# A choice product on 64 columns, and a last block computed in two halves, in an attention and expert kernel

## The chip, the cores and the metric

The kernel runs on one core of a Trainium2 chip. The metric is the device time of one execution in microseconds (us). The time before is 420.47 us, the median of 3 runs (420.36 to 421.25).

## The reference

For each of 8 batches there are 8 heads with 576 tokens of 64 values, and 32 "packs". Two softmax attentions come first: packs over keys and values, then queries over the packed result. Their output, 576 tokens of 512 values for each batch, goes into a layer of 8 experts.

```
p_packed = sm_attn(p, k, v)
x        = sm_attn(q, p_packed, p_packed)          # [8, 576, 512] after the heads are joined
logits   = x @ w_gate;  local = sigmoid(x @ w_local)
for each batch, token after token:
    fresh = argmax(logits[s])
    e     = fresh if s == 0 or local[s] < 0.5 else the token before's e
    out[s] = softmax(logits[s])[e] * (relu(x[s] @ w1[e]) @ w2[e])
```

`w1` is 512 x 1024 and `w2` 1024 x 512 for each expert.

## The kernel before

Batches run one after the other, with the attention of later batches woven between the expert products of the current one. The expert of a batch's first token is found early and its `w1` and `w2` are loaded by an address in a register. The whole batch is computed with that expert; tokens that need another one are counted as strays, and a block behind a branch (L1259, not entered here unless there are strays) repairs them. So every engine loads the count (L1258, a load into a register), compares and branches at L1259, and then runs the closing waits (L1346).

**The choice product.** For batches 2 to 7 `first_choice` (L715 to L743) takes the attention of token 0, normalizes it, turns it with one DVE transpose into the tile `first`, and multiplies it on TensorE with the gate weights (L737): two matmuls in float32, one for each Q (group of four heads). Each is two instructions in the profile, each with its own weight load. The stationary operand is `first[:, Q:Q + 4]`, four slots of 32 columns, of which only the first column matters: the one row of `ep` that is read is row 0. `first` has NQ + 3 = 5 slots, so that four are there from Q = 1; the last three are zero for good (memset at L257).

**The expert layer.** For each batch there are two halves of tokens, and in each half 8 chunks of 128 hidden columns. `layer1` makes a chunk's hidden values (L1013: six matmuls of 320 or 256 columns), `relu` splits them into a high and a low part (ACT L1024, DVE L1028), and `layer2` multiplies them with the chunk's `w2` (three matmuls for a block of 128 tokens: high by high, high by low, low by high, L1041, all of 512 columns). `BLOCKS` names the blocks of a half: 0, 1 and the mixed block 4 (L1046, L1050) in the first, 2 and 3 in the second. Each block has one PSUM bank that accumulates over the 8 chunks. Chunk c's second layer follows chunk c + 1's first layer.

**The end.** In the last half of the last batch the chunks before last and last are ordered by block: block 2 of both, then block 3 of both (L1138). When a block is complete, `store` scales it by the gate (block 2 on DVE, L1076; block 3 on ACT, L1074) and issues its DMA: on the queue of SP, except block 3 of the last batch, which goes on ACT's (L1085). The count of strays (`count_strays`) is put in ahead of these matmuls.

**What orders the work.** The program's order is written out when the kernel is built: `weave` keeps a model of the engines' clocks (`Clock`) and takes, step by step, the generator whose data are due. A matmul's price goes by its output columns; it is priced as a small tile, with a charge for the change, if it has 64 or fewer rows on one side and its output has not exactly 64 rows (L108). `hold` keeps free PSUM banks back for the blocks of a half that begins (L1115). All engines run their instructions in this order. Lines that the change touches: L37, L256, L738, L1034 to L1050, L1055 to L1087, L1104, L1115, L1131, L1138.

Of the kernel before, what the change touches and what calls it, by code (L numbers as in the profile page):

```python
# [8 lines left out]
F32 = mybir.dt.float32  # L9
# [13 lines left out]
NQ = H // HQ  # L23
# [10 lines left out]
WIDE = GROUP * 5  # L34
ROWS = ((0, 128), (128, 128), (WIDE, 128), (WIDE + 128, 128), (256, TAIL))
BLOCKS = ((0, 1, 4), (2, 3))

RATIO, BACKLOG, CREDIT, DEBT, AHEAD = 0.7, 800.0, 1000.0, 1300.0, 2

# [132 lines left out]
def packed_attn_moe_kernel(  # L172
# [80 lines left out]
    for x in v_rest + a_rest:  # L253
        nc.gpsimd.memset(x[TAIL:128], 0.0)

    first = const.tile([128, NQ + 3, 32], F32, name="first")  # L256
    nc.gpsimd.memset(first, 0.0)  # L257
    some = const.tile([1, 1], I32, name="some")
    v0_all = const.tile([128, B], F32, name="v0_all")
# [118 lines left out]
    def begin(b, st, early=False):  # L378
        st["b"], st["early"] = b, early

        st["second"] = isinstance(b, int) and b == 1
        st["pairs"] = st["early"] or st["second"]
        st["pick"] = isinstance(b, int) and b < PICK
        st["gate"] = gate_all[b % 3 if isinstance(b, int) else 0]
        st["ppT"] = [None] * NQ
        st["wp"], st["w2s"], st["at"] = [], [], b if isinstance(b, int) else -1
        st["quads"] = [0, 0]
        st["wq"] = st["passed"] = st["asked"] = st["scored"] = st["weighed"] = st["valued"] = st["raised"] = st["peeked"] = 0
# [326 lines left out]
    def first_choice(st, sT):  # L715

        m, nm, sm = (tile_([128, NQ], F32, x) for x in ("em", "enm", "esm"))
        yield need(*sT.values())
        for Q in range(NQ):
            nc.vector.reduce_max(out=m[:, Q:Q + 1], in_=sT[Q][:, 0, 0], axis=AX.X)  # L720
        nc.vector.tensor_scalar(out=nm, in0=m, scalar1=-SCALE, scalar2=None, op0=ALU.mult)
        yield need(nm)
        es = tile_([128, NQ, 32], F32, "es")
        for Q in range(NQ):
            nc.scalar.activation(
                out=es[:, Q], in_=sT[Q][:, 0, 0], func=AF.Exp, bias=nm[:, Q:Q + 1], scale=SCALE, accum_out=sm[:, Q:Q + 1],
            )
        st["peeked"] = 1
        yield need(es, sm)
        nc.vector.tensor_scalar(out=sm, in0=sm, scalar1=1e-9, scalar2=None, op0=ALU.add)  # L730
        nc.vector.reciprocal(out=sm, in_=sm)
        nc.vector.tensor_tensor(out=es, in0=es, in1=sm.unsqueeze(2).broadcast_to([128, NQ, 32]), op=ALU.mult)
        nc.vector.transpose(out=first[:, 0:NQ].rearrange("a q n -> a (q n)"), in_=es.rearrange("a q n -> a (q n)"))
        yield need(first, st["gs"], banks=1)
        ep = bank()
        for Q in range(NQ):
            nc.tensor.matmul(  # L737
                out=ep[:, 0:GW], lhsT=first[:, Q:Q + 4].rearrange("a q n -> a (q n)"), rhs=st["gs"][:, Q, 0:GW],  # L738
                start=(Q == 0), stop=(Q == NQ - 1),
            )  # L740
        yield need(ep)
        yield from first_code(st, ep[0:1, 0:E])
        give(ep)  # L743
# [276 lines left out]
    def relu(t, half, h, done):  # L1020
# [10 lines left out]
        give(t)  # L1031
        done.add("h")

    def layer2(c, h, w, st, i):  # L1034
        if c == 0:
            st["acc", i] = bank()
        acc = st["acc", i]
        if i < 4:
            hs = [h[:, x + 128 * (i % 2):x + 128 * (i % 2) + 128] for x in (0, WIDE + TAIL)]
            for n, (hi, wi) in enumerate(((0, 0), (0, 1), (1, 0))):  # L1040
                nc.tensor.matmul(  # L1041
                    out=acc, lhsT=hs[hi], rhs=w[:, wi],
                    start=(c == 0 and n == 0), stop=(c == NC - 1 and n == 2),
                )
        else:
            nc.tensor.matmul(  # L1046
                out=acc, lhsT=h[:, 256:WIDE + TAIL], rhs=w[:, 0],
                start=(c == 0), stop=False, skip_group_check=True,
            )
            nc.tensor.matmul(  # L1050
                out=acc[0:TAIL], lhsT=h[:, 256:WIDE], rhs=w[:, 1],
                start=False, stop=(c == NC - 1), skip_group_check=True,
            )

    def store(b, st, i, mask=None):  # L1055

        acc, pe = st["acc", i], st["pe"]
        yield need(acc)
        o = tile_([128, DM], F32, "o")
        row, rows = ROWS[i]  # L1060
        if i == 4:

            o2 = tile_([TAIL, DM], F32, "o2", "o")
            nc.scalar.activation(out=o2, in_=acc[TAIL:128], func=AF.Copy, scale=pe[TAIL:128, i:i + 1])
            yield need(o2)
            nc.vector.scalar_tensor_tensor(
                out=o[:TAIL], in0=acc[0:TAIL], scalar=pe[0:TAIL, i:i + 1], in1=o2, op0=ALU.mult, op1=ALU.add,
            )
        elif i == 0:

            nc.scalar.activation(out=o[:, 0:256], in_=acc[:, 0:256], func=AF.Copy, scale=pe[:, i:i + 1])
            nc.vector.tensor_scalar(out=o[:, 256:DM], in0=acc[:, 256:DM], scalar1=pe[:, i:i + 1], scalar2=None, op0=ALU.mult)
        elif i == 3:
            nc.scalar.activation(out=o, in_=acc, func=AF.Copy, scale=pe[:, i:i + 1])  # L1074
        else:
            nc.vector.tensor_scalar(out=o, in0=acc, scalar1=pe[:, i:i + 1], scalar2=None, op0=ALU.mult)  # L1076
        give(acc)
        dst = at(out, b)[row:row + rows]
        if mask is not None:
            new, o = o, tile_([128, DM], F32, "o")  # L1080
            nc.sync.dma_start(out=o[:rows], in_=dst)
            nc.vector.copy_predicated(
                out=o[:rows], mask=mask[:rows, i:i + 1].broadcast_to([rows, DM]), data=new[:rows],
            )
        queue = nc.scalar if isinstance(b, int) and b == B - 1 and i == 3 else nc.sync  # L1085
        clock.rate = 300.0
        queue.dma_start(out=dst, in_=o[:rows])  # L1087

    def chunks(todo, aside, mask=None):

        def second(last, blocks):
            b, st, half, c, h, done = last
            for i in blocks:
                yield need(h, *st["w2s"][c:c + 1], banks=1 if c == 0 else 0, first=True,
                           when=lambda: "h" in done and len(st["w2s"]) > c and (c < NC - 1 or "pe" in st))
                yield need(st["w2s"][c])
                layer2(c, h, st["w2s"][c], st, i)
                if c == NC - 1:  # L1100
                    aside(store(b, st, i, mask))
            if c == 0:
                hold[0] = 1
            if half == 1 and i == BLOCKS[half][-1]:  # L1104
                give(st["w2s"][c])

        last = None
        for b, st in todo:
            for half in range(2):
                for c in range(NC):  # L1110
                    if c % 2 == 0:
                        yield need(when=lambda: st["wq"] > c // 2 and st["quads"][half] == NQ)
                    if c == 0:
                        at_batch[0] = b
                        hold[0] = 1 + len(BLOCKS[half])  # L1115
                    hi, lo = (x[:, 0, 256 * (c % 4 // 2) * st["early"]:] for x in st["wp"][c // 4])
                    if mask is None and (b, half, c) == (0, 0, 2):
                        give(warm_ps)
                    yield need(hi, lo, *(x[:, WIDE * half:WIDE * half + 256] for y in ("a2h", "a2l") for x in st[y]), banks=1, first=True)
                    h, done = tile_([128, 2 * WIDE], F32R, "h"), set()  # L1120
                    aside(relu(layer1(c, half, st), half, h, done))
                    st["begun"] = True
                    st["passed"] += 1
                    if half == 1:
                        if c % 4 == 3:
                            give(*st["wp"][c // 4])
                        if c == NC - 1:
                            give(*st["a2h"], *st["a2l"])
                    end = half == 1 and c == NC - 1 and b is todo[-1][0]
                    if last is not None and not end:  # L1130
                        yield from second(last, BLOCKS[last[2]])  # L1131
                    before, last = last, (b, st, half, c, h, done)

        if mask is None:
            ending.append(True)
            yield need()
            aside(count_strays())
        for x, blocks in ((before, (2,)), (last, (2,)), (before, (3,)), (last, (3,))):  # L1138
            yield from second(x, blocks)

    def count_strays():

# [208 lines left out]
```

## Time and profile before

| | |
|---|---|
| median of 3 runs | 420.47 us (420.36 to 421.25) |
| the profiled execution | 422.95 us, its span 421.1 us |
| granted TensorE clock | 0.999 |
| busy: PE, PEld, DVE, ACT, POOL | 97%, 77%, 70%, 43%, 11% of the span |
| instructions | 10055 |

The profile shows one execution. PE is TensorE's matmul track, PEld its weight loads, which run beside matmuls; DVE is VectorE, ACT ScalarE, POOL GpSimd, SP the engine that issues most DMAs. A letter q behind an engine marks its queue or sequencer: DMA issues, waits, branches. A matmul's duration holds the time through the array, so matmuls in a row overlap in the record, and the distance of their starts tells what one costs.

### The profile page before, as it was taken

Reading aid. Unit: us, or ns where it says so; the run is one execution under the profiler, and the core shown is the slowest. Engines: PE = TensorE matmul, PEld = TensorE weight load, DVE = VectorE, ACT = ScalarE, POOL = GpSimd, SP = SyncE. Lnnn points to the kernel's source line nnn. Section 1 sums busy time; section 2 is a strip of 40 time slices with the busy share of each in tenths; the row PEclk is TensorE's granted clock in tenths of the full one; section 3 lists DMA queues with packets and bytes.
Section 4 is the critical chain, followed back from the end, with each engine's and each line's share of the span. In section 5 each row is a group of like instructions: output and inputs, shape, how many; then the busy total and the mean of one; then the engine's idle time right before and its main releaser. Section 6 shows DMA issues by size and latency. Waiting matters only on the chain.

```text
span 421.1 us, 10055 instructions
## 1 busy us (share of the span) xinstructions
PE 409.9 (97%) x3810; PEld 322.3 (77%) x3816; DVE 296.3 (70%) x915; ACT 181.6 (43%) x443; POOL 46.9 (11%) x66
## 2 busy tenths in 40 slices
PE   6999999999999999999999999999999999999995
PEld 3656677867887788878887788877887788878883
DVE  1587458796596968978496978978497987765221
ACT  2464553456244644254244643354343653453221
POOL 2003320253102000200003000300003000300000
PEclk9999999999999999999999999999999999999999
DMA  7859993999996699938986599929997500823021
GB/s 205 250 180 321 258 129 94 307 161 220 139 188 238 208 167 139 324 86 243 133 171 261 198 173 130 333 81 247 128 146 296 150 2 2 296 93 125 0 65 58
DMA packets 161160, 73.11 MB, mean 174 GB/s; under 512 B 125768, under 2 KB 141128, under 8 KB 161104
## 3 DMA queue, kind: packets, MB, share of 16 engines
q1 hardware_dynamic: 160624, 72.04, 74.9%
q8 instruction: 32, 0.52, 0.6%
q10 hardware_dynamic: 480, 0.35, 0.3%
q14 instruction: 24, 0.20, 0.2%
HBM read 62.94 MB, written 9.44 MB: 172 GB/s over the span
## 4 chain that ended last, share of the span: by engine, by line
PE 87%; DMA 8%; SPq 2%; DVE 1%; issue 1%; ACT 1%; DVEq 0%; ACTq 0%
PE bank L1041 40%; PE bank L1013 23%; PE bank L1046 4%; PE bank L1050 3%; DMA qn<-in_q_dram 3%; PE bank L971 3%; PE bank L560 2%; DMA kv<-in_q_dram 2%; PE bank L496 2%; PE bank L534 2%; PE bank L611 2%; DMA w1t<-in_moe_w_dram 2%; DMA qt<-in_k_dram 2%; PE bank L801 1%; PE bank L226 1%; PE bank L441 1%
## 5 line engine op out<-in xcount | busy, mean ns | idle before, releaser
L1041 PE MATMUL bank<-w2s,h 128*128 128x512 f32 x768 | 205.3, 399 | 0.2 <-ACT h L1024 0.2
L1041 PEld LDWEIGHTS bank<-w2s,h 128*128 128x128 f32 x768 | 135.8, 188 | 29.3 <-ACT wph L983 5.0
L1028 DVE SCALAR_TENSOR_TENSOR h<-bank,h 128x256 fp32r<-128x256 f32 x192 | 61.4, 347 | 61.4 <-ACT h L1024 60.2
L1024 ACT ACTIVATE h<-bank 128x256 fp32r<-128x256 f32 (+1 forms) x128 | 52.7, 412 | 114.0 <-PE bank L1013 112.2
L1013 PEld LDWEIGHTS bank<-a2h,wph 128*128 128x128 f32 x256 | 46.6, 188 | 16.7 <-issue 2.8
L1013 PE MATMUL bank<-a2h,wph 128*128 128x320 f32 (+1 forms) x256 | 57.0, 303 | 0.1
L1013 PE MATMUL bank<-a2h,wpl 128*128 128x320 f32 (+1 forms) x256 | 55.9, 298 | 0.5 <-DVE wpl L986 0.5
L676 POOL TENSOR_TENSOR a2l<-a2t,a2h 128x576 fp32r<-128x576 f32 (+2 forms) x17 | 23.3, 1376 | 294.8 <-ACT a2h L673 294.8
L1013 PE MATMUL bank<-a2l,wph 128*128 128x320 f32 (+1 forms) x256 | 54.5, 294 | 0.0
L999 ACT CAST w2s<-w2raw 128x512 fp32r<-128x512 f32 x64 | 39.0, 625 | 7.6 <-DMA w2raw<-in_moe_w_dram 7.6
L1013 PEld LDWEIGHTS bank<-a2h,wpl 128*128 128x128 f32 x256 | 40.9, 188 | 1.5 <-DVE wpl L986 1.5
L1013 PEld LDWEIGHTS bank<-a2l,wph 128*128 128x128 f32 x256 | 41.0, 188 | 0.0
L1001 DVE TENSOR_TENSOR w2s<-w2raw,w2s 128x512 fp32r<-128x512 f32 x50 | 33.2, 681 | 2.9 <-ACT w2s L999 2.9
L1046 PE MATMUL bank<-w2s,h 128*128 128x512 f32 x64 | 26.9, 420 | 0.0
L1050 PE MATMUL bank<-w2s,h 128*64 128x512 f32 x64 | 25.2, 393 | 0.0
L983 ACT CAST wph<-bank 128x512 fp32r<-128x512 f32 x28 | 15.2, 600 | 22.3 <-PE bank L971 22.3
L1001 POOL TENSOR_TENSOR w2s<-w2raw,w2s 128x512 fp32r<-128x512 f32 x14 | 18.2, 1308 | 25.0 <-ACT w2s L999 17.3
L631 DVE STREAM_TRANSPOSE sT<-bank 128x288 f32<-128x288 f32 (+2 forms) x36 | 13.2, 418 | 9.0 <-ACT gate L629 8.5
L504 DVE TENSOR_SCALAR_CACHE_REDUCE a<-bank 128x288 f32<-128x288 f32 x32 | 13.3, 453 | 7.3 <-PE bank L496 7.3
L986 DVE TENSOR_TENSOR wpl<-bank,wph 128x512 fp32r<-128x512 f32 x28 | 18.4, 680 | 0.0
L595 DVE STREAM_TRANSPOSE qn<-qn 128x1152 f32<-128x1152 f32 x12 | 16.3, 1361 | 0.0
L463 DVE STREAM_TRANSPOSE qn<-qn 128x1152 f32<-128x1152 f32 x12 | 16.3, 1360 | 0.0
(161 smaller groups left out, 462.9 us busy)
## 6 DMA issues: line engine op xcount, KB each, us to landing
w2raw<-in_moe_w_dram SPq DMA_DIRECT2D x64, 256.0 KB, 6.6
w1t<-in_moe_w_dram SPq DMA_DIRECT2D x14, 1024.0 KB, 5.2
kv<-in_v_dram SPq DMA_DIRECT2D x16, 512.0 KB, 5.9
out_dram<-o SPq DMA_DIRECT2D x31, 256.0 KB, 3.2
qn<-in_k_dram SPq DMA_DIRECT2D x24, 288.0 KB, 6.7
qn<-in_q_dram SPq DMA_DIRECT2D x24, 288.0 KB, 7.2
w1t<-in_moe_w_dram SPq DMA_DIRECT2D x4, 512.0 KB, 5.2
kw<-in_k_dram SPq DMA_DIRECT2D x3, 512.0 KB, 7.2
```

What stands on the lines that cost most here:

```text
L463: nc.vector.transpose(out=kT, in_=kT)
L595: nc.vector.transpose(out=qT, in_=qT)
L676: eng.tensor_tensor(out=a2l, in0=a2t, in1=a2h.bitcast(F32), op=ALU.subtract)
L986: nc.vector.tensor_tensor(out=lo[fh][:, Q], in0=ts[fh, Q], in1=hi[fh][:, Q].bitcast(F32), op=ALU.subtract)
L999: nc.scalar.copy(out=w[:, 0], in_=raw)
L1001: (nc.gpsimd if st["pick"] and not st["early"] or st["early"] and c > 1 else nc.vector).tensor_tensor(out=w[:, 1], in0=raw, in1=w[:, 0].bi ...
L1013: nc.tensor.matmul(out=t[:, :GROUP * (m1 - m0)], lhsT=st["wp"][c // 4][wi][:, Q, fs], rhs=a2[ai][Q][:, GROUP * m0:GROUP * m1], start=(n == ...
L1024: nc.scalar.activation(out=h[:, :w], in_=t[:, :w], func=AF.Relu)
L1028: nc.vector.scalar_tensor_tensor(out=h[:, dst:dst + z - a], in0=t[:, a:z], scalar=0.0, in1=h[:, a:z].bitcast(F32), op0=ALU.max, op1=ALU.su ...
L1041: nc.tensor.matmul(out=acc, lhsT=hs[hi], rhs=w[:, wi], start=(c == 0 and n == 0), stop=(c == NC - 1 and n == 2),)
L1046: nc.tensor.matmul(out=acc, lhsT=h[:, 256:WIDE + TAIL], rhs=w[:, 0], start=(c == 0), stop=False, skip_group_check=True,)
L1050: nc.tensor.matmul(out=acc[0:TAIL], lhsT=h[:, 256:WIDE], rhs=w[:, 1], start=False, stop=(c == NC - 1), skip_group_check=True,)
```

## The change

The choice product takes two slots as its stationary operand in place of four, and writes 64 rows in place of 128. `first` loses two slots that were always zero.

The last batch has blocks 2, 3 and 5 in its second half. Blocks 3 and 5 are the two halves, 256 columns each, of what was block 3, each with a PSUM bank of its own. Through all 8 chunks block 3's three matmuls of 512 columns become three of 256 for block 3 and three of 256 for block 5. Each is scaled by an ACT instruction of 256 columns and stored by a DMA of 128 KB: block 3 on SP's queue, block 5 on ACT's. The loop at the end goes through the blocks of the batch in order: 2, 3, 5.

```diff
+LAST_BLOCKS = ((0, 1, 4), (2, 3, 5))
...
-    first = const.tile([128, NQ + 3, 32], F32, name="first")
+    first = const.tile([128, NQ + 1, 32], F32, name="first")
...
+        st["blocks"] = LAST_BLOCKS if isinstance(b, int) and b == B - 1 else BLOCKS
...
-                out=ep[:, 0:GW], lhsT=first[:, Q:Q + 4].rearrange("a q n -> a (q n)"), rhs=st["gs"][:, Q, 0:GW],
+                out=ep[0:64, 0:GW], lhsT=first[:, Q:Q + 2].rearrange("a q n -> a (q n)"), rhs=st["gs"][:, Q, 0:GW],
...
+    def columns(st, i):
+
+        return slice(0, DM) if 5 not in st["blocks"][1] or i not in (3, 5) else slice(0, 256) if i == 3 else slice(256, DM)
...
-        if i < 4:
+        if i != 4:
+            cols = columns(st, i)
...
-                    out=acc, lhsT=hs[hi], rhs=w[:, wi],
+                    out=acc[:, cols], lhsT=hs[hi], rhs=w[:, wi, cols],
...
-        row, rows = ROWS[i]
+        cols, n = columns(st, i), min(i, 3) if i != 4 else 4
+        row, rows = ROWS[n]
...
-        elif i == 3:
-            nc.scalar.activation(out=o, in_=acc, func=AF.Copy, scale=pe[:, i:i + 1])
+        elif n == 3:
+            nc.scalar.activation(out=o[:, cols], in_=acc[:, cols], func=AF.Copy, scale=pe[:, 3:4])
...
-        queue = nc.scalar if isinstance(b, int) and b == B - 1 and i == 3 else nc.sync
+        queue = nc.scalar if i == 5 else nc.sync
         clock.rate = 300.0
-        queue.dma_start(out=dst, in_=o[:rows])
+        queue.dma_start(out=dst[:, cols], in_=o[:rows, cols])
...
-                        hold[0] = 1 + len(BLOCKS[half])
+                        hold[0] = 1 + len(st["blocks"][half])
...
-        for x, blocks in ((before, (2,)), (last, (2,)), (before, (3,)), (last, (3,))):
-            yield from second(x, blocks)
+        for i in last[1]["blocks"][1]:
+            yield from second(before, (i,))
+            yield from second(last, (i,))
```

## Rows read from the trace of the kernel before

**Rows 1.** The page's section 4: shares of the chain that ended last, by engine.
```profile
PE 87%; DMA 8%; SPq 2%; DVE 1%; issue 1%; ACT 1%; DVEq 0%; ACTq 0%
```
**Rows 2.** Stretch, length, busy us of PE, PEld, DVE, ACT, POOL, clock, DMA share, GB/s.
```profile
117.00:416.00 299.00, 298.93 (x2614) 242.61 (x2612) 221.15 (x652) 127.28 (x307) 19.66 (x24) 1.00 0.71 163
```
**Rows 3.** Chain that ended last, in order of time: start us, us, what.
```profile
399.39 0.23 PE bank L1050
...
410.83 1.39 PE bank L1041 x6
412.21 0.70 PE bank L1013 x6
...
413.03 2.91 PE bank L1041 x12
...
415.96 0.69 ACT o L1074
```
**Rows 4.** Lines L1258 and L1259: count, ns min/median/max, first and last start.
```profile
L1258 SPq TENSOR_LOAD <-some x1: 278/278/278, 415.7 to 415.7; - x1
...
L1259 SPq EVENT_SEMAPHORE  x9: 17/17/17, 419.2 to 419.8; - x9
...
L1259 ACTq EVENT_SEMAPHORE  x2: 17/17/17, 418.1 to 418.2; - x2
...
L1259 SPq COMPARE_BRANCH  x1: 73/73/73, 416.3 to 416.3; - x1
L1259 ACTq COMPARE_BRANCH  x1: 68/68/68, 417.7 to 417.7; - x1
```
**Rows 5.** Line L737, the choice product: its weight loads.
```profile
L737 PEld LDWEIGHTS bank<-gate,first x24: 187/190/192, 117.4 to 355.0; 128*128 128x128 f32 x24
```
**Rows 6.** Timeline of weight loads around batch 7's choice product: start, us, what.
```profile
354.74 0.19 PEld L737 LDWEIGHTS bank<-gate,first 128*128 128x128 f32 x1
...
354.85 0.30 PEld L737 LDWEIGHTS bank<-gate,first 128*128 128x128 f32 x2
...
355.07 0.19 PEld L1013 LDWEIGHTS bank<-a2h,wph 128*128 128x128 f32 x1
```
**Rows 7.** Timeline of weight loads of 64 and of 32 columns.
```profile
15.79 0.53 PEld L307 LDWEIGHTS bank<-ident,gate_rows 8*64 8x64 f32 x8
...
22.80 0.20 PEld L787 LDWEIGHTS bank<-gate,et 128*32 128x32 f32 x4 [0.38 <-DVE et L784]
```
**Rows 8.** Groups of weight loads: busy us, mean ns, idle before.
```profile
L1050 PEld LDWEIGHTS bank<-w2s,h 128*64 128x64 f32 x64 | 8.7, 136 | 2.1
...
L307 PEld LDWEIGHTS bank<-ident,gate_rows 8*64 8x64 f32 x8 | 0.5, 143 | 0.0
...
L787 PEld LDWEIGHTS bank<-gate,et 128*32 128x32 f32 x8 | 0.4, 110 | 0.7 <-DVE et L784 0.4 <-ACT o L1071 0.4
```
**Rows 9.** Timeline of PE where products on 32 columns follow full ones.
```profile
157.71 0.63 PE L1041 MATMUL bank<-w2s,h 128*128 128x512 f32 x2
158.27 1.20 PE L611 MATMUL bank<-qn,ppT 64*32 64x288 f32 x32
```
**Rows 10.** Line L1071, an ACT scaling of 256 columns out of PSUM.
```profile
L1071 ACT ACTIVATE o<-bank,pe x8: 466/475/475, 66.9 to 398.5; 128x256 f32<-128x256 f32 x8
```
**Rows 11.** Timeline of the last two stores' issues.
```profile
415.34 0.34 SPq L1087 DMA_DIRECT2D out_dram<-o  x1
...
416.68 0.39 ACTq L1087 DMA_DIRECT2D out_dram<-o  x1
```
**Rows 12.** Busy time by stretch after the last store's issue, columns as in rows 2.
```profile
417.50:418.00 0.50, 0.00 (x0) 0.00 (x0) 0.00 (x0) 0.00 (x0) 0.00 (x0) 1.00 0.86 324
...
418.50:419.00 0.50, 0.00 (x0) 0.00 (x0) 0.00 (x0) 0.00 (x0) 0.00 (x0) 1.00 0.08 20
```
**Rows 13.** Timeline of weight loads at the start, with what ended the wait.
```profile
3.75 0.23 PEld L477 LDWEIGHTS bank<-ident,p_in 128*128 128x128 f32 x1 [0.27 <-POOL first L257]
...
4.89 1.14 PEld L441 LDWEIGHTS bank<-ident,kw 128*128 128x128 f32 x6 [0.48 <-DMA kw<-in_k_dram]
```

More of the change, by code (lines that the diff above doesn't have):

```diff
@@ L1103, in second @@
                 hold[0] = 1
-            if half == 1 and i == BLOCKS[half][-1]:
+            if half == 1 and i == st["blocks"][half][-1]:
                 give(st["w2s"][c])
@@ L1130, in chunks @@
                     if last is not None and not end:
-                        yield from second(last, BLOCKS[last[2]])
+                        yield from second(last, last[1]["blocks"][last[2]])
                     before, last = last, (b, st, half, c, h, done)
```

## The prediction

> **What bounds the kernel now.** I read the chain of waits first: 87% of it is PE [rows 1]. Then the busy time by stretch: from 117 to 416 us PE is busy 298.93 of 299.00 us, with the granted clock at 1.00 [rows 2]. So from the first choice product on nothing that another engine or a DMA does holds PE up, and what is taken out of PE's stream there comes off the end, unless the data then come late. What follows PE's last matmul is not on PE: the chain by time ends with twelve matmuls up to 413.03 + 2.91 = 415.94 us and ACT's scaling of 0.69 from 415.96 [rows 3], ACT issues the last store at 416.68 [rows 11], and the span ends at 421.1. Those last 5 us need a second look, because two chains run there side by side: ACT's store until it lands, and SP's way out of the program.
>
> SP issues its last store at 415.34 [rows 11], loads the count of strays at 415.7, branches at 416.3, and shows nothing until its closing waits begin at 419.2 [rows 4]. From the branch on that is some 2.8 us. ACT has the same steps: its branch at 417.7, its waits already at 418.1 [rows 4], 0.4 us. SP's first wait is the one that comes latest, and the rest of SP's closing steps follow it one by one to the end of the span. The data of ACT's store meanwhile flow at a DMA share of 0.86 from 417.5 and are down to 0.08 from 418.5 [rows 12]. So I read SP's exit as what ends the span, with the last store's landing just ahead of it.
>
> The row leaves open why SP stands still. The Trainium skill (Runtime: NRT & Kernel Launch, Instruction fetch mechanics) says that a taken branch whose target lies outside the small window of fetched instructions has to wait for a DMA to bring the page. That the engines differ so much here, 2.8 us against 0.4, agrees with a window that holds the target for one of them and not for the other; no row names the fetch. By that rule the whole 2.8 us starts when SP branches, and moves with it; were it a wait for ACT's store instead, it would get shorter with the change. These are the forecast and the first rival below.
>
> **The change part by part.**
>
> *Choice product, 64 columns.* It runs 6 times, 4 weight loads each (24) [rows 5]. The moving side is 9 columns, so the loads set the pace. In batch 7 they start at 354.74, 354.85, one between, and the next product's at 355.07 [rows 6]: three distances in 0.33 us, 0.11 each (the first load hides behind the matmul ahead of it). For 64 columns the nearest case is L307, eight loads in a row in 0.53 us of 0.143 each [rows 7, 8]: (0.53 - 0.143) / 7 = 0.055 us. The two ends: 32 columns, four in 0.20 us of 0.110 each, so (0.20 - 0.11) / 3 = 0.03 [rows 7, 8]; and no change, 0.11. I take 0.055, since it has the very number of columns; also L1050's loads of 64 columns take 136 ns against 190 for L737's 128 [rows 8, 5]. Gain: 3 x 0.055 = 0.165 us for a batch, times 6 = 0.99 us (ends 0 and 3 x 0.08 x 6 = 1.44). All of it lies on PE, which never waits there [rows 2]. A loss is possible if 64 columns count as a small tile: where products on 32 columns follow full ones, the last full matmul starts at 157.71 + 0.23 = 157.94 and the next product at 158.27, 0.33 later in place of 0.23 [rows 9], so a switch costs 0.10. L1050 speaks against that: 64 columns, and it takes 0.23 in the chain like its neighbours [rows 3]. I take no switch.
>
> The choice itself is known 0.16 us sooner, so its `w1` loads go out sooner by as much; since PE does not wait for them now, I cost that at nothing. The planner sees the same columns and, with 64 rows out, the same kind of price, so I expect the same order up to the last half. The shorter memset of `first` can help only at the start, where a weight load waits for it until 3.75 us [rows 13]. Right behind, PE waits for the DMA of k until 4.89 [rows 13], which covers it: nothing.
>
> *Block 3 as two blocks, in the chunks.* In each of 8 chunks three matmuls of 512 columns become six of 256. Six of 512 take 1.39 us, so three take 0.695; six of 256 in the first layer, which are float32r with a weight load each as here, take 0.70 [rows 3]. That is +0.01 a chunk; six chunks lie ahead of the end, +0.06 us. The rows show this very operation, so I bound it only by their last digit, 0 to +0.12. One more PSUM bank is held, 3 of 8; nothing else wants banks there but the first layer and the count of strays: nothing.
>
> *The end.* All times now stand on the clock of the kernel before, so that the PE gain is added last. The twelve matmuls end at 415.94 + 0.02 = 415.96 with block 5, and block 3 ends 0.70 before it, at 415.26. ACT scales block 3 from 415.28 in 0.47 us (256 columns take 475 ns, not half of 0.69) [rows 10], to 415.75. In the old profile the DMA went out 0.03 after ACT's end (415.96 + 0.69 = 416.65, issue at 416.68). So SP issues block 3's store at 415.78. SP has block 2's store at 415.34 and 0.34 us of issuing behind it, free at 415.7: it waits about 0.1 us for ACT, then issues for some 0.35 us. Queued behind that instruction on SP are the load of the count, the branch and the closing waits, which everything at the end waits for. They followed the issue at 415.34 before and follow the one at 415.78 now: +0.44 us. Lower end: 0, or below, if SP's stall is not counted from its branch.
>
> ACT begins block 5 at 415.98, ends at 416.45 and issues at 416.48, 0.20 us earlier than before, with half the bytes. Its store lands some 0.2 to 0.7 us earlier (0.7 if half of the data time of about 1 us [rows 12] goes as well). Behind SP's exit, this is worth nothing.
>
> *Sum.* -0.99 + 0.06 + 0.44 = -0.49 us. The profiled execution took 422.95 us (span 421.1) and would take 422.46. It is 2.48 above the median of the runs; I carry the difference over: 420.47 - 0.49 = 420.0 us.
>
> **The rivals.**
>
> *The store's landing ends the span, or SP's stall does not begin at the branch.* For it: the last data of ACT's store are through shortly before SP moves [rows 12, 4]. Against it: the first of SP's nine closing waits is the late one, and it comes ahead of others that follow in even steps. Then the tail gains 0.2 to 0.6, say 0.3: -0.99 + 0.06 - 0.3 = -1.23, 419.2 us.
>
> *64 columns make TensorE switch its tiling,* at L737, twice in each batch (in and out), 0.10 each: 6 x 0.20 = 1.2 us against the gain of 0.99. With chunks and tail: -0.99 + 1.2 + 0.06 + 0.44 = +0.71, 421.2 us, slower than before. It decides from 0.04 us a switch on (0.49 / 12). For it: the switch is plain in rows 9. Against it: L1050 passes without one, though it is float32r and 512 columns wide.
>
> *The shorter weight load doesn't shorten the product:* 0 + 0.06 + 0.44 = +0.50, 421.0 us. For it: L307 has 8 active rows only. Against it: L1050's loads at 128 rows are shorter too [rows 8]. The Trainium skill (TensorE: Matmul & The Clock Gate, Weight-path perf modes) has a rule that would do this: the fast weight load needs the full 128 columns, so 64 would lose it. It also says that float32 never has it, and the trace agrees that no load here is faster for being full (190 ns full, 136 ns half).
>
> **How the numbers follow.** Forecast 0.60, landing or stall 0.22, tiling switch 0.07, no shorter product 0.05, and 0.06 for what I don't see (code and tile addresses move, the order in the last half), both ways alike. What a measurement of this kernel can tell from no change is about 0.2%, 0.84 us, that is below 419.63 or above 421.31. The forecast lies within: its own range is 419.5 to 420.5 us, and some 0.09 of its 0.60 falls below 419.63 with the scatter of runs. The landing rival lies below but for 0.04, 0.18; unseen 0.02: faster 0.29. Slower: half of the tiling switch with its scatter, 0.03, the unseen and the tail of the rest, 0.04: 0.07. Same 0.64. The range goes from 419.0, in the landing rival, to 421.1, short of the tiling switch.
>
> **What would show it.** The three distances of weight loads at L737 should be 0.055, and the matmul behind it should come 0.16 sooner, in all six batches; PE's last matmul should end at about 415.0. The six matmuls of a chunk's blocks 3 and 5 should take 1.40 to 1.41. SP's last issue should stand at about 414.9 (415.78 less 0.93), its branch at 415.8, and the stall after it should again be 2.8 us; the closing waits then begin near 418.7. The prediction is wrong if that stall is shorter than 2.3 us, if the matmul behind L737 starts late, or if PE shows waits in the last half.

## The result and the profile after

| | median | lowest to highest | ratio to before |
|---|---|---|---|
| before | 420.42 us (6 runs) | 419.73 to 421.25 | |
| after | 422.96 us (6 runs) | 422.31 to 423.25 | 1.0054 (95%: 1.0042 to 1.0066) |

The change costs 0.5% by the ratio, 2.5 us between the medians. The profiled execution took 422.86 us with a span of 421.1 us. That is the span of the first profile of before as well, but that profile was a late one. A second profile of the kernel before (experiment e1) has a span of 418.5 us, so below before is read from e1 wherever a time since the start counts, and from the rows ahead of the prediction where only distances count.

First the choice product of batch 7, in the timeline of PE (start in us, us, what), after and then e1 [rows 5, 6]:

```profile
352.56 0.40 PE L1057 MATMUL bank<-w2s,h 128*64 128x512 f32 x1
352.89 0.40 PE L739 MATMUL bank<-gate,first 128*64 128x9 f32 x4
353.22 0.39 PE L1015 MATMUL bank<-a2h,wph 128*128 128x256 f32 x1
```
```profile
351.95 0.40 PE L1050 MATMUL bank<-w2s,h 128*64 128x512 f32 x1
352.18 0.51 PE L737 MATMUL bank<-gate,first 128*128 128x9 f32 x4
352.54 0.37 PE L1013 MATMUL bank<-a2h,wph 128*128 128x256 f32 x1
```

From the matmul ahead of the choice product to the one behind it the change takes 0.66 us, before took 0.59. The choice product starts 0.33 after the matmul ahead of it in place of 0.23. The weight loads of after there, in the timeline of PEld, and the choice product's own in e1:

```profile
352.34 0.14 PEld L1057 LDWEIGHTS bank<-w2s,h 128*64 128x64 f32 x1
352.89 0.31 PEld L739 LDWEIGHTS bank<-gate,first 128*64 128x64 f32 x4 [0.42 <-DVE h L1030]
353.22 0.30 PEld L1015 LDWEIGHTS bank<-a2h,wph 128*128 128x128 f32 x2
```
```profile
351.95 0.65 PEld L737 LDWEIGHTS bank<-gate,first 128*128 128x128 f32 x4
```

Four loads in 0.31 us of 0.138 each are (0.31 - 0.138) / 3 = 0.057 apart, about as forecast. But the first no longer starts together with the matmul ahead of it (352.56); it starts with its own matmul at 352.89. In e1 the same first load starts with the matmul ahead, both at 351.95. The load that follows the choice product is later as well, 0.16 us behind its last load in place of 0.11. The releaser that the row names is not the cause: the operand was turned by 352.32, over half a microsecond before, as the timeline of DVE of after shows:

```profile
352.07 0.25 DVE L735 STREAM_TRANSPOSE first<-es 128x64 f32<-128x64 f32 x1
```

The other five batches show the same. Where the matmul ahead has 512 columns, the choice product starts 0.33 us after it in place of 0.23; where it has 256 (two batches), 0.21 in place of 0.12. Each costs 0.06 us more than in e1, the six together 0.37.

Second the last half, in the chain of waits of after [rows 3]: one chunk's second layer, and the end.

```profile
408.37 0.71 PE bank L1015 x6
409.08 1.42 PE bank L1048 x9
...
411.32 2.94 PE bank L1048 x18
414.26 0.02 issue
414.29 0.47 ACT o L1082
```

The chunk takes 1.42 us in place of 1.39, the end 2.94 in place of 2.91. PE is through at 414.26. Three views of after follow: the issues of the three last stores in the timeline of SP and ACT [rows 11]; SP's instructions at the register load and the branch, with ns min/median/max and the first and last start [rows 4]; and SP's waits, who waited for whom, in us:

```profile
413.64 0.34 SPq L1095 DMA_DIRECT2D out_dram<-o  x1
...
414.08 1.39 SPq L1095 DMA_DIRECT2D out_dram<-o  x1
...
414.79 0.39 ACTq L1095 DMA_DIRECT2D out_dram<-o  x1
```
```profile
L1267 SPq TENSOR_LOAD <-some x1: 531/531/531, 415.5 to 415.5; - x1
...
L1268 SPq EVENT_SEMAPHORE  x9: 17/17/17, 419.1 to 419.7; - x9
...
L1268 SPq COMPARE_BRANCH  x1: 73/73/73, 416.4 to 416.4; - x1
```
```profile
SPq L1268 <- SPq L1268: 2.7, 1, 2.7
```

SP's issue of block 3's half store takes 1.39 us where its others take 0.34. The branch comes at 416.4, 2.1 us after the last matmul (before: 0.4), and 2.7 us later the closing waits begin. From the last matmul to the end of the span it is 6.8 us; before it was 5.2.

### The profile page after: what moved, and what is told of

Same layout as the page of the kernel before. It is cut to its first block, busy times and chain, and to the rows that moved or that the text cites. A ratio compares the mean times of both kernels' runs of the same rounds, so it can differ in the third digit from the quotient of the medians.

```text
span 421.1 us, 10108 instructions
## 1 busy us (share of the span) xinstructions
PE 410.4 (97%) x3834; PEld 323.1 (77%) x3840; DVE 296.0 (70%) x915; ACT 182.1 (43%) x444; POOL 46.9 (11%) x66
## 4 chain that ended last, share of the span: by engine, by line
PE 92%; DVE 3%; DMA 2%; ACT 1%; issue 0%; SPq 0%; DVEq 0%; ACTq 0%
PE bank L1048 43%; PE bank L1015 25%; PE bank L1053 4%; PE bank L1057 4%; PE bank L973 3%; PE bank L562 2%; PE bank L498 2%; PE bank L613 2%; PE bank L536 2%; DMA qt<-in_k_dram 2%; PE bank L803 1%; PE bank L227 1%; PE bank L443 1%; PE bank L944 1%; DMA p_in<-in_p_dram 1%; PE bank L739 0%
## 5 line engine op out<-in xcount | busy, mean ns | idle before, releaser
L1048 PE MATMUL bank<-w2s,h 128*128 128x512 f32 (+1 forms) x792 | 205.4, 392 | 0.0
L1048 PEld LDWEIGHTS bank<-w2s,h 128*128 128x128 f32 x792 | 138.0, 188 | 28.4 <-ACT wph L985 5.0
L1053 PE MATMUL bank<-w2s,h 128*128 128x512 f32 x64 | 26.9, 421 | 0.0
```

The lines of the kernel that those rows point to most:

```text
L1048: nc.tensor.matmul(out=acc[:, cols], lhsT=hs[hi], rhs=w[:, wi, cols], start=(c == 0 and n == 0), stop=(c == NC - 1 and n == 2),)
L1053: nc.tensor.matmul(out=acc, lhsT=h[:, 256:WIDE + TAIL], rhs=w[:, 0], start=(c == 0), stop=False, skip_group_check=True,)
```

## The experiments

All are read against before as it ran beside them on the same chip. "E" is the end of the last matmul; a time behind E does not depend on how the execution began.

**e1: before again.** No edit.

> The kernel before, unchanged, for a second profile. The first profiled execution took 422.95 us where the runs have a median of 420.42, and in it the first DMA of k landed 1.7 us later than in the changed kernel. Theory 1 (the two parts of the change cost 2.5 us and the first profile of before was a late one): the span is near 418.6 us, the product that follows the first choice product of batch 2 starts about 2.2 us earlier than in the first profile, and the end after the last matmul (5.2 us) is the same. Rival (the late start belongs to the profiled executions of both kernels): the span is again near 421.1.

Measured: 420.34 us, span 418.5 us. In the first profile the matmul that waits for the first small DMA of k started at 8.75 us, here at 7.25 (timeline of PE, e1):

```profile
7.25 0.33 PE L449 MATMUL bank<-ident,qt 128*128 128x128 f32 x1 [1.48 <-DMA qt<-in_k_dram]
```

By 45 us the difference has grown to 2.5 us and stays. The chain of waits of e1 has the last matmuls, so that E is 413.38, and the end comes 5.1 us behind it:

```profile
410.47 2.91 PE bank L1041 x12
```

Theory 1 holds. The 2.5 us by which the first profiled execution lay above the median came from its first 45 us, so carrying that difference over did no harm.

**e2: 64 columns alone.**

```diff
-    first = const.tile([128, NQ + 3, 32], F32, name="first")
+    first = const.tile([128, NQ + 1, 32], F32, name="first")
-                out=ep[:, 0:GW], lhsT=first[:, Q:Q + 4]...
+                out=ep[0:64, 0:GW], lhsT=first[:, Q:Q + 2]...
```

> The choice product on 64 columns alone; the last block as before. Theory 1 (float32 products on 64 columns make TensorE switch its tiling, about 0.1 us in and 0.1 us out, against 0.11 to 0.16 us of shorter weight loads): 6 x 0.08 = +0.5 us against before, about 420.9. Rival as predicted (the shorter loads come off in full): -1.0 us, about 419.5.

Measured: 421.17 us against 420.53, ratio 1.0014 (1.0001 to 1.0026), +0.6 us. The interval only just leaves out no change, but the trace agrees: in batch 7 the distance across the choice product is again 0.65, and from the matmul ahead of the first choice product (batch 2) to E it is 298.9 us (115.09 to 414.03), against 298.4 in e1 (114.93 to 413.37), +0.5. The time is that of theory 1, and the prediction's gain does not exist. That TensorE switches a tiling is the theory's name for the late start; no row names it.

**e3: the halves alone.** The rest of the change, with the choice product on 128 columns.

> The last block of the last batch in two accumulators alone; the choice product on 128 columns as before. Theory 1 (SP's way out is later by the added store: +0.4 us for waiting on ACT, +1.05 for an issue that takes 1.39 us where the others take 0.34, +0.2 behind it): +0.1 on TensorE and +1.65 at the end, together +1.8 us against before. Rival as predicted (the issue takes 0.34 us): +0.5 us.

Measured: 422.23 us against 420.53, ratio 1.0049 (1.0030 to 1.0069), +1.7 to +2.1 us. SP's half store takes 1.44 us to issue, its branch comes at 415.5 with E at 413.43, its waits at 418.5:

```profile
413.24 1.44 SPq L1095 DMA_DIRECT2D out_dram<-o  x1
```

With e2's +0.6 the two parts add up to the whole.

**e4: 96 columns.** As e2, with three slots (`first[:, Q:Q + 3]`, 96 rows out).

> The choice product on 96 columns (three slots, 96 rows out), the rest as before. If the switch comes from an operand that fits a smaller tile (64 or 32 columns), 96 columns have none and their weight loads are closer together, about 0.083 us in place of 0.11: 6 x 3 x 0.027 = -0.5 us against before. If any operand of fewer than 128 columns costs the switch: +0.6 us. If a load takes as long as for 128: no change.

**e11: 68 columns.** The stationary operand is cut out of the flat `first` (four slots), 68 rows out:

```diff
+                out=ep[0:68, 0:GW], lhsT=first.rearrange("a q n -> a (q n)")[:, 32 * Q:32 * Q + 68], ...
```

> The choice product on 68 columns, the rest as before. If the switch goes with operands of at most 64 columns and the distance of weight loads with their columns (0.11 at 128, 0.055 at 64), 68 columns have no switch and 0.059 between loads: 6 x 3 x 0.052 = -0.94 us against before, the best of all versions. If a part of the array that isn't whole costs the switch as well: +0.5 us.

Measured: e4 420.03 us against 420.53, ratio 0.9996 (0.9980 to 1.0012), no difference by the runs; e11 419.04 us against 420.64, ratio 0.9961 (0.9941 to 0.9981). The timelines of PE, e4 and then e11:

```profile
351.75 0.40 PE L1050 MATMUL bank<-w2s,h 128*64 128x512 f32 x1
351.98 0.43 PE L737 MATMUL bank<-gate,first 128*96 128x9 f32 x4
352.26 0.36 PE L1013 MATMUL bank<-a2h,wph 128*128 128x256 f32 x1
```
```profile
350.63 0.39 PE L1050 MATMUL bank<-w2s,h 128*64 128x512 f32 x1
350.87 0.36 PE L737 MATMUL bank<-gate,first 128*68 128x9 f32 x4
351.08 0.37 PE L1013 MATMUL bank<-a2h,wph 128*128 128x256 f32 x1
```

Across the choice product it is 0.51 us with 96 columns and 0.45 with 68, where 128 take 0.59 and 64 take 0.66. The start is 0.23 to 0.24 after the matmul ahead in both, as with 128. So the shorter loads do come off, by columns, and the late start is there at 64 and not at 68. The six distances of e11 together are 0.89 us shorter than in e1, and from the matmul ahead of the first choice product to E it is 297.5 us (114.45 to 411.95) against 298.4, 0.9 less; the rest of the 1.6 us between the medians lies within the scatter of the runs. e11 beats both kernels.

**e5: both half stores on ACT's queue.** As e3, with block 3's store on ACT's queue too.

> Halves as in the change, choice product on 128 columns as before, and both half stores on ACT's queue, so that SP has only block 2's store at the end. Theory 1 (what costs is SP's added store, ahead of SP's way out): SP's first closing wait comes 3.2 us after the last matmul as before, and the time is before plus 0.1 for the chunks. Rival (a half store that follows another store on any queue is slow to issue): ACT's second issue takes over 1 us, its landing becomes the last thing, and the time is over 1 us above before.

Measured: 421.69 us against 421.23, ratio 1.0014 (0.9990 to 1.0039). SP's waits begin 3.1 us behind E as before, the span ends 5.1 behind E. Theory 1 holds: with SP's queue as before, the loss at the end is gone. It brings no gain either. ACT issues the first half for 0.39 us, scales the second only behind that, and issues it 0.83 us behind E, later than before's whole store (0.75). That second issue takes 0.46 us, so the rival's 1 us did not come.

**e6: block 3 whole, on SP's queue.**

```diff
-        queue = nc.scalar if isinstance(b, int) and b == B - 1 and i == 3 else nc.sync
+        queue = nc.sync
```

> The kernel before with block 3's store, whole, on SP's queue in place of ACT's: SP has an added store of the old shape, issued 0.75 us after the last matmul. Theory 1a (the issue is slow for the half shape): it takes 0.34 us, SP's branch comes 1.3 us later than before, the stall after it is again 2.7 us, and the time is +1.3 us. Theory 1b (the issue waits until the store ahead of it on the queue has landed, 1.3 us after the last matmul): it takes about 0.55 us, +1.5 us. Rival (SP's stall ends on a landing, not a fixed time behind its branch): under +0.5 us.

Measured: 422.22 us against 421.23, ratio 1.0026 (0.9996 to 1.0055), which by the runs alone is not clear of no change. The issue takes 0.71 us, the branch comes at 417.4 with E at 415.32, the waits begin at 420.4, 3.0 us later; the span ends 7.1 us behind E in place of 5.2. SP's stall goes with its branch, so the last rival fails. But 0.71 us fits neither 1a nor 1b:

```profile
416.07 0.71 SPq L1087 DMA_DIRECT2D out_dram<-o  x1
```

**e7 and e8: which store is slow to issue.** Both as e3; e7 has block 2's store on ACT's queue and block 3's half on SP's, e8 block 3's half on ACT's and block 5's half on SP's.

> Halves as in the change, choice product on 128 columns, block 2's store on ACT's queue and block 3's half store on SP's, with no store close ahead of it there. If the issue on SP is slow because of the store just ahead on the same queue, it takes 0.34 us, and SP's branch comes 1.1 us earlier than with the halves alone (about 1.05 us after the last matmul). If it is slow because of its shape, or because SP's queue is slow at this point, it takes 1.4 us again.

> Halves as in the change, choice product on 128 columns, block 3's half on ACT's queue and block 5's half on SP's, 0.54 us after the last matmul in place of 0.17 before it. If an issue waits for the landing of the store ahead on its queue (first data landed 1.3 us after the last matmul), it takes about 0.75 us; if the half shape costs 1.05 us by itself, 1.4 us; if only stores less than half a microsecond apart are slow, 0.34 us.

Measured: e7 421.47 us and e8 421.60, one run each, against 421.23. In the timelines of SP and ACT, e7's issues, then e8's second issue on SP (E at 413.84 and 413.29):

```profile
413.24 0.39 ACTq L1095 DMA_DIRECT2D out_dram<-o  x1
...
414.18 0.34 SPq L1095 DMA_DIRECT2D out_dram<-o  x1
414.55 0.95 ACTq L1095 DMA_DIRECT2D out_dram<-o  x1
```
```profile
414.12 0.33 SPq L1095 DMA_DIRECT2D out_dram<-o  x1
```

In e7 the half on SP takes 0.34 us with nothing ahead of it on SP, and the second store on ACT's queue, 1.3 us behind block 2's, takes 0.95. In e8 the half follows block 2's store on SP by 1.4 us and takes 0.33, before that store has landed. So neither the shape nor SP by itself makes an issue slow. e8's 0.33 is what the reading by distance gives (only stores less than half a microsecond apart are slow), but the slow issues of e7 and e6, 1.3 us behind the store ahead, go against it.

What does fit is an instruction fetch. In each of these traces a 16 KB packet of queue q8 starts shortly before E, in the stretch behind TensorE's own branch. Most such packets are not a branch's: the profile's page of before counts 32 of them over the whole kernel. In the trace's packets the one near E ends at 415.10 us in after, 414.31 in e3, 416.41 in e6, 415.11 in e7. The held issues end at 415.47, 414.68, 416.78 and 415.50, 0.37 to 0.39 us later each time. ACT's second issue in e5 fits as well: it is held for a moment (0.46 us) and ends at 415.82, 0.38 behind its packet. In e8 the packet ended at 414.00, and the issue at 414.12 was not held. Packets of the other instruction queue, q14, show no such fixed distance: they end 0.10, 0.19, 0.37 and 0.59 us ahead of the four issues. The DMA view of after from 413.9 to 416.0 and of e8 from 412.9 to 415.0 shows the packet (packets, MB, share of 16 engines' time):

```profile
q8 instruction: 1, 0.02, 3.1%
```
```profile
q8 instruction: 1, 0.02, 2.8%
```

3.1% of 16 engines in 2.1 us is 1.04 us of one engine. As I read it (the trace does not name the engine of a packet), the packet keeps one DMA engine busy; that engine still has to move its part of the store ahead, and the next store on the same queue isn't taken in until it does. A queue with nothing ahead isn't held (ACT's first issue in e5 and e8, 0.39 us, in the midst of the fetch). The kernel before shows the same in its body: an issue of `w2` at 378.99 us takes 1.04 us in place of 0.34, with one such packet between 378.4 and 380.1 (its timeline of SP, and its DMA view):

```profile
378.99 1.04 SPq L895 DMA_DIRECT2D w2raw<-in_moe_w_dram  x1
```
```profile
q8 instruction: 1, 0.02, 4.3%
```

The packet is not the only thing that goes with a slow issue. In the same trace a store of the body at 86.91 us takes 2.17 us to issue with no such packet near it, behind issues of about 2 us each on the same queue.

**e9 and e10: without the branch.** Both leave out the load of the count of strays, the branch (with the hint that announces it) and the repair behind it; e9 is otherwise before, e10 is otherwise e3.

> The kernel before without the branch behind which strays are repaired: the count is not loaded into registers, nothing branches, the repair is left out. Theory 1 (SP's stall follows its branch): SP begins its closing waits right behind its last issue and is then held by the last store's landing alone, so the span ends about 4.7 us after the last matmul in place of 5.2. Rival (the stall is a wait for the store or for something else at the end): 5.2 again.

> The last block in two halves (choice product on 128 columns), without the branch and the repair. Theory 2 (SP's second issue is held up by the 16 KB instruction fetch that TensorE's branch sets off, which occupies a DMA engine that still has to move part of block 2's store): no branch, no fetch, and the issue takes 0.34 to 0.39 us; the stores land about 0.4 us sooner than without halves, the span ends about 4.2 us after the last matmul. Rival (the issue is slow because it follows another store on SP's queue by less than half a microsecond): 1.4 us again, and a landing near 2.5 us after the last matmul.

Measured, in one run each, against 420.64: e9 420.22 us with E at 414.45 and the span at 418.4, e10 419.42 us with E at 414.13 and the span at 417.6. SP's waits in e9, then e10's second issue in the timeline of SP and SP's waits in e10:

```profile
SPq L1278 <- DMA out_dram<-o: 3.1, 1, 3.1
```
```profile
413.94 0.38 SPq L1095 DMA_DIRECT2D out_dram<-o  x1
```
```profile
SPq L1287 <- DMA out_dram<-o: 2.1, 1, 2.1
```

Now SP's long wait is for the store, where it was SP's own before. The span ends 4.0 us behind E in e9 (the closing steps are fewer too, so this is more than the 0.5 us expected) and 3.5 in e10. Same shapes, same distance of the two issues (0.43 us) as in e3, no packet of q8 near the end, and the issue takes 0.38 us. So theory 2 holds as far as one run can show it: without the branch the packet is gone, and with it the held issue. And here the halves gain what they were worth at the landing: 0.5 us at the end, of which the chunks take back 0.2.

## Why the prediction was wrong, point by point

- *PE bounds the kernel and what is added to its stream comes off or on the end.* Right: what the six choice products lose or gain is still there at E, +0.5 us in e2 and -0.9 in e11.
- *The distance of the loads, 0.055 us.* Right: 0.057.
- *"I take no switch."* This is the step that failed first. The choice product on 64 columns starts 0.10 us later, and the product behind it begins its loads 0.05 later too; together the six lose 0.06 us each, 0.37 in all, and to E it is +0.5 us in place of -0.99. (The other 0.1 is spread over the stretches between them.) One of the prediction's own signs of being wrong, a late start of the matmul behind L737, had come. The tiling rival had this loss, priced at +0.2 a batch less the gain of 0.165; I gave it 0.07. I ruled it out by L1050, which also has 64 columns. But L1050 is float32r and the choice product float32, and L307, which gave the distance, lies between products on 32 and 128 columns, so it shows nothing of a product on 64 columns between full ones. That a row has the same number of columns was not enough. e4 and e11 show that the delay is gone from 68 columns on. Why float32r at 64 columns has none is open: the choice product in float32r was not tried.
- *The chunks, +0.01 each.* Small in the sum but outside its bounds: 1.42 in place of 1.39, about +0.03 each, and 2.94 in place of 2.91 at the end, some +0.2 us in all.
- *SP's way out ends the span and moves with the branch.* Right: the stall is 2.6 to 3.0 us long in after, e3, e6 and e7, where the branch stands 1.3 to 2.1 us behind E, and 2.8 in e1, where it stands at 0.4; it is gone without the branch in e9. By the Trainium skill (Runtime: NRT & Kernel Launch, Instruction fetch mechanics) a taken branch to a page outside the window waits for a fetch. The trace agrees in that the stall starts with the branch, but no row shows that SP waits for a page.
- *The wait for ACT, +0.44 us.* Right: SP's second issue begins 0.18 us before E, where its only one began 0.60 before (412.78 in e1).
- *The issue itself, 0.34 us.* The second step that failed, mis-sized by 1.05 us: 1.39. I took the price from issues that had no instruction fetch beside them, though the profile's page lists an instruction queue and the body of before had a held issue of 1.04 us. Behind it the register load took 0.53 us in place of 0.28 and came with a later branch, another 0.25; its cause is open.
- *The sum.* Forecast -0.99 + 0.06 + 0.44 = -0.49. Measured +0.5 + 0.2 + 0.4 + 1.05 + 0.25 = +2.4, against 2.54 between the medians. The forecast's 420.0 us, with its range up to 421.1, is missed by both failed steps: 1.5 us on the choice product and 1.05 on the issue.
- *The landing rival.* Wrong as the cause (SP was last), but its price was near: without the branch the halves gain 0.5 us.

## What to carry to other kernels

When the time of an operand's load is to be saved by fewer columns, look for a row with the same type and the same kind of product, and try more than one width: here 68 columns of 128 gave the gain that 64 turned into a loss. Before work is put on a queue at the end of a program, write down everything that stands behind it on that engine, a branch above all, and price its issue from a row that has the same neighbours, instruction fetches among them. A store that lands sooner is worth nothing as long as another engine leaves the program later.

## What the runs showed of the hardware that I had not expected

- A float32 product on 64 stationary columns began 0.33 us after the matmul of 512 columns ahead of it; on 68, 96 and 128 columns 0.23 to 0.24 (after, e11, e4, e1). A float32r product on 64 columns showed no such delay (L1050 in e1, 0.24).
- Weight loads of 128, 96, 68 and 64 columns behind one another were 0.108 to 0.112, 0.081 to 0.085, 0.058 to 0.062 and 0.054 to 0.059 us apart over the six batches (e1, e4, e11, after).
- Six issues of a DMA behind another on the same queue ended 0.37 to 0.39 us after a 16 KB instruction packet did, the longest of them at 1.44 us in place of 0.34: those of after, e3, e5, e6 and e7, and the one of `w2` in the body of before. The same issue of `w2` took 0.87 us in e1 and 0.93 in after, and ended 0.30 and 0.28 behind its packet.
- From SP's branch to its next instruction it was 2.6 to 3.0 us, from DVE's 2.9 to 3.5 (413.5 to 416.9 in after); ACT's took 0.5 at the same place (415.8 to 416.3 in after).
